# Second products 32 steps behind the first, w_in decoded first and without GpSimd, 25 attention batches ahead of the loop

## The chip, the core and the metric

The kernel runs on one core of a Trainium2 chip: TensorE (matrix products, into PSUM), VectorE and ScalarE (elementwise work, both read PSUM), GpSimd (elementwise work on SBUF), and SyncE, whose queue issues nearly all transfers between DRAM and SBUF. Each engine takes its instructions in the order in which the program gives them. The metric is the time of one execution in microseconds (us), the median of several.

## What is computed

A retention layer (attention with a decay in place of the softmax) over 8 sequences of 576 tokens and 8 heads of 64, and two MLPs on its 4608 tokens, with 512 inputs and 2048 inner columns each:

```
scores = (q @ k.T) / sqrt(64)                       # per batch and head
ret    = (scores * where(i >= j, gamma_h ** (i - j), 0)) @ v
x = ret, heads side by side                         # 4608 x 512
h = x @ w_in;   x = (h * sigmoid(1.702 * h)) @ w_out    # first MLP
h = x @ w_in2;  y = (h - tanh(h)) @ w_out2              # second MLP
```

The weights reach the kernel as 64-bit floats, so that it must turn them into 32-bit values itself; this is called decoding here.

## The kernel before, in words

**Pieces.** Each operand of a large product is split into a high part and a low rest (`xh`, `xl`; the halves of `wi`, `wos` and `g`), and three products of parts are summed. The tokens come in 9 blocks of 512, the inner columns in 16 groups of 128. A step `s` is one block `j` and one group `f` of one MLP, 288 in all. In a step `mm_in` (L356 to L367) makes the first product `h` in 12 matmuls of 512 columns, `act_a` (L369) the activation `t` out of it (a tanh on ScalarE and one instruction on VectorE in the first MLP, three and five in the second), `act_b` (L388) splits `t` into `g` (a copy on ScalarE, a subtraction on VectorE), and `mm_out` (L394 to L407) adds the second product of the step `LAG` = 2 steps ago to four PSUM accumulators, in 12 matmuls. `evac` (L409) empties these after 16 steps: into DRAM after the first MLP, from where `x2_load` and `x2_split` take the block for the second, into the output after the second.

**Attention.** A batch is half a tile of 128 tokens (four heads); there are 72, 8 to a block. Each has scores (L251), a state (L266), the part of the result from the state (L237) and from the masked scores `p` (L302). VectorE makes `p` (L274), the new state (L284 or L288) and `xl` (L317), ScalarE `xh` (L316) and the state's copy `sbd` (L324). `at_scale` (L201) scales queries and keys of a tile on GpSimd, L209 and L212. Nine batches stand ahead of the main loop, the others go in at every second step, as late as the blocks allow.

**Decoding.** There are 64 chunks of 128 x 512 values: two MLPs, 16 groups, `w_in` (c = 0) and `w_out` (c = 1), which take turns. A chunk is loaded by `wload` (L94), then goes through `dec_a` (VectorE L104, ScalarE Relu L106, VectorE L107), `dec_a2` (VectorE L112), `dec_b` (VectorE L118, GpSimd multiplication L123) and `dec_c` (ScalarE copy L139, GpSimd subtraction L140). `dec_piece` hands these out in thirds of a chunk, three chunks being in work at a time. During the first block each step takes two chunks, since each step needs its own `wi` and its own `wos`; the second MLP's chunks follow later, one every three steps, and go to DRAM. The 16 `wi` stay in SBUF; `wos` are stored to DRAM too and loaded again for each later block by `wo_load` (L177), through a ring of 4 buffers, on SyncE's queue.

**Order.** The order of instructions on each engine is the one in which the program writes them. PSUM has `pat` (2 banks), two `h` (1 each) and four accumulators; ahead of the loop three pairs of banks `pe` stand in place of `h` and the accumulators.

Of the kernel before, what the change touches and what calls it, by code (L numbers as in the profile page):

```python
# [16 lines left out]
P = 128  # L17
# [22 lines left out]
N_WARM = 12  # L40


@with_exitstack
def kernel(
# [12 lines left out]
    LAG = 2  # L57
# [3 lines left out]
    wos_p = ctx.enter_context(tc.tile_pool(name="wos", bufs=4))  # L61
    x_p = ctx.enter_context(tc.tile_pool(name="x", bufs=2))
    at_p = ctx.enter_context(tc.tile_pool(name="at", bufs=2))
    p_p = ctx.enter_context(tc.tile_pool(name="p", bufs=4))
    g_p = ctx.enter_context(tc.tile_pool(name="g", bufs=LAG + 1))
# [3 lines left out]
    ps_a = ctx.enter_context(tc.tile_pool(name="ps_a", bufs=1, space=bass.MemoryType.PSUM))  # L69

# [45 lines left out]
    def dec_b(m, f, c):  # L116
# [6 lines left out]
        nc.gpsimd.tensor_tensor(out=o, in0=z.bitcast(F32), in1=e.bitcast(F32), op=ALU.mult)  # L123
        half[m, f, c] = o

    def dec_c(m, f, c):
        o = half.pop((m, f, c))
        if c == 1:
            if m == 0:
                s = wos[f] = wos_p.tile([P, 2, DM], F32R, tag="wos", name="wos")  # L130
            else:
                s = st_p.tile([P, 2, DM], F32R, tag="stg", name="w2s", bufs=3)
        elif m == 0:
            s = wts.tile([P, 2, KD, P], F32R, tag=f"wi{f}", name="wi")
            win[f] = s
        else:
            s = st_p.tile([P, 2, KD, P], F32R, tag="stg", name="w2s", bufs=3)
        sv = s if c == 1 else s.rearrange("p a k c -> p a (k c)")
        nc.scalar.activation(out=sv[:, 0], in_=o, func=ACTF.Copy)  # L139
        nc.gpsimd.tensor_tensor(out=sv[:, 1], in0=o, in1=sv[:, 0].bitcast(F32), op=ALU.subtract)  # L140
        if c == 1 or m == 1:
# [4 lines left out]

    chunks = []
    for m in range(2):
        for f in range(NF + 1):
            chunks += ([(m, f, 0)] if f < NF else []) + ([(m, f - 1, 1)] if f else [])  # L150
# [8 lines left out]
    def dec_piece():  # L159
        n, k = divmod(n_dec[0], 3)  # L160
        if n >= len(chunks) + 2:
            return
        n_dec[0] += 1
        if k == 0:
            dec_load(n + 2)
            if n >= 2:
                dec_c(*chunks[n - 2])
            if 1 <= n <= len(chunks):
                dec_b(*chunks[n - 1])
        elif n < len(chunks):  # L170
            (dec_a if k == 1 else dec_a2)(*chunks[n])

    def dec_slot():
        for _ in range(3):
            dec_piece()
# [150 lines left out]
    def attn_step(b, ps=None):  # L326
# [4 lines left out]
        if now:  # L331
# [3 lines left out]
            if early:  # L335
                bat_p(b)
# [238 lines left out]
```

## Time and profile before

| | us |
|---|---|
| median of 3 executions (1793.1 to 1794.53) | 1793.56 |
| the profiled execution | 1794.65 |
| its span in the trace | 1792.9 |
| TensorE busy in the span | 1749.3 (98%) |
| VectorE busy | 1076.5 (60%) |
| ScalarE busy | 717.9 (40%) |
| GpSimd busy | 329.4 (18%) |

The shares are means over stages that differ, so they are to be read by stretches. In rows of the trace PE is TensorE, PEld its weight loads, DVE VectorE, ACT ScalarE, POOL GpSimd, SPq SyncE's queue. Every row names a line of the kernel before, what is written `<-` what is read, and a duration. A bracket at the end of a row is the idle time of the engine before it, and whose work ended that.

### The profile page before, as it was taken

To read this page: it belongs to the slowest core of one execution; us is meant where nothing else is said; L and a number is where in the kernel's file an instruction comes from. 1 tells how busy PE (TensorE), PEld (TensorE's weight loads), DVE (VectorE), ACT (ScalarE), POOL (GpSimd) and SP (SyncE) were. 2 spreads that over 40 slices of the span, in tenths; PEclk is the share of its full clock that TensorE was granted. 3 is DMA by queue.
4 is the path that set the end of the run, shared out by engine and by line. 5 is a ranking of instruction groups with operands and counts; after the bars stand their busy time and mean duration, and the time that the engine had idled before them with its cause. 6 is when DMAs were issued, how large, how long until landed. Compare 5 with 4: busy or idle time off the path is not lost.

```text
span 1792.9 us, 22946 instructions
## 1 busy us (share of the span) xinstructions
PE 1749.3 (98%) x8920; PEld 1430.8 (80%) x8920; DVE 1076.5 (60%) x1690; ACT 717.9 (40%) x1299; POOL 329.4 (18%) x240
## 2 busy tenths in 40 slices
PE   7878999999999999999999999999999999999999
PEld 5656788888888888888888888888888888888887
DVE  6899744444444445433322577777777777777776
ACT  2434433333333323323222444454445444545444
POOL 4666422223223223210001010101000000000000
PEclk7988999999999999999999999999999999999999
DMA  5555745555455545633355524342434233424232
GB/s 215 169 188 187 259 165 179 185 188 203 155 218 186 186 158 189 222 127 133 119 197 190 188 95 141 103 144 94 141 100 147 94 141 99 148 95 141 95 129 83
DMA packets 75421, 277.63 MB, mean 155 GB/s; under 512 B 8752, under 2 KB 8880, under 8 KB 69680
## 3 DMA queue, kind: packets, MB, share of 16 engines
q1 hardware_dynamic: 74736, 276.07, 44.0%
q8 instruction: 71, 1.16, 0.3%
q14 instruction: 38, 0.31, 0.1%
q10 hardware_dynamic: 576, 0.08, 0.0%
HBM read 232.08 MB, written 44.04 MB: 154 GB/s over the span
## 4 chain that ended last, share of the span: by engine, by line
PE 90%; DVE 8%; issue 1%; DMA 0%; ACT 0%; POOL 0%; SPq 0%; DVEq 0%; POOLq 0%
PE h L364 41%; PE acc L407 22%; PE acc L405 20%; DVE z L107 2%; PE pat L251 2%; DVE g L392 2%; PE pat L302 1%; DVE e L118 1%; PE pat L237 1%; PE pat L266 1%; DVE e L104 1%; DVE t L374 1%; DMA at<-in_attn_dram 0%; DVE z L112 0%; DVE p L274 0%
## 5 line engine op out<-in xcount | busy, mean ns | idle before, releaser
L364 PE MATMUL h<-xh,wi 128*128 128x512 f32 x2304 | 768.6, 395 | 28.6 <-ACT wi L139 22.2
L364 PEld LDWEIGHTS h<-xh,wi 128*128 128x128 f32 x2304 | 437.6, 190 | 129.2 <-ACT wi L139 25.7
L364 PE MATMUL h<-xl,wi 128*128 128x512 f32 x1152 | 453.2, 393 | 0.0
L405 PE MATMUL acc<-g,wos 128*128 128x512 f32 x1728 | 424.1, 394 | 0.6 <-DVE g L392 0.5
L407 PE MATMUL acc<-wos,g 128*128 128x512 f32 x1728 | 415.0, 389 | 0.0
L405 PEld LDWEIGHTS acc<-g,wos 128*128 128x128 f32 x1728 | 319.4, 188 | 75.6 <-issue 9.4
L407 PEld LDWEIGHTS acc<-wos,g 128*128 128x128 f32 x1728 | 324.1, 188 | 67.8 <-DVE g L392 0.4
L392 DVE TENSOR_TENSOR g<-t,g 128x512 fp32r<-128x512 f32 x288 | 238.3, 827 | 209.4 <-ACT g L391 209.4
L391 ACT ACTIVATE g<-t 128x512 fp32r<-128x512 f32 x288 | 181.3, 630 | 433.1 <-DVE t L386 354.4
L364 PEld LDWEIGHTS h<-xl,wi 128*128 128x128 f32 x1152 | 219.3, 190 | 45.6
L374 DVE SCALAR_TENSOR_TENSOR t<-t,h 128x512 f32<-128x512 f32 x144 | 98.3, 682 | 157.4 <-ACT t L373 156.9
L438 POOL TENSOR_TENSOR xl<-x2s,xh 128x512 fp32r<-128x512 f32 x36 | 46.5, 1293 | 774.2 <-ACT xh L437 774.2
L381 DVE TENSOR_TENSOR t<-h,t 128x512 f32<-128x512 f32 x144 | 99.6, 692 | 98.1 <-ACT sq L379 98.1
L373 ACT ACTIVATE t<-h 128x512 f32<-128x512 f32 x144 | 86.0, 598 | 173.4 <-PE h L364 172.1
L317 DVE TENSOR_TENSOR xl<-pat,xh 128x256 fp32r<-128x256 f32 x64 | 27.1, 423 | 208.2 <-ACT xh L316 208.2
L140 POOL TENSOR_TENSOR w2s<-z,w2s 128x512 fp32r<-128x512 f32 x32 | 53.8, 1683 | 383.9 <-ACT w2s L139 383.9
L316 ACT ACTIVATE xh<-pat 128x256 fp32r<-128x256 f32 x64 | 24.5, 382 | 238.6 <-PE pat L302 238.6
L386 DVE COPY_PREDICATED t<-sq,pl 128x512 f32<-128x512 int32 x144 | 109.2, 759 | 4.9
L123 POOL TENSOR_TENSOR z<-z,e 128x512 f32<-128x512 f32 x64 | 100.1, 1564 | 35.3 <-DVE e L118 35.3
L380 ACT ACTIVATE pl<-sq,abias 128x512 f32<-128x512 f32 x144 | 104.1, 723 | 4.8
L383 DVE SCALAR_TENSOR_TENSOR pl<-pl,sq 128x512 f32<-128x512 f32 x144 | 99.7, 692 | 9.4
L378 ACT ACTIVATE t<-h 128x512 f32<-128x512 f32 x144 | 86.1, 598 | 42.8 <-PE h L364 42.8
(61 smaller groups left out, 1174.6 us busy)
## 6 DMA issues: line engine op xcount, KB each, us to landing
wos<-wd SPq DMA_DIRECT2D x272, 512.0 KB, 4.4
at<-in_attn_dram SPq DMA_DIRECT2D x35, 1024.0 KB, 4.9
stg<-in_w_dram SPq DMA_DIRECT2D x64, 512.0 KB, 5.5
wd<-w2s SPq DMA_DIRECT2D x32, 512.0 KB, 3.0
x<-o SPq DMA_DIRECT2D x36, 256.0 KB, 3.6
x2s<-x SPq DMA_DIRECT2D x9, 1024.0 KB, 6.7
out_dram<-o SPq DMA_DIRECT2D x36, 256.0 KB, 2.3
wd<-wos SPq DMA_DIRECT2D x16, 512.0 KB, 2.9
```

The lines of the kernel that those rows point to most:

```text
L123: nc.gpsimd.tensor_tensor(out=o, in0=z.bitcast(F32), in1=e.bitcast(F32), op=ALU.mult)
L364: nc.tensor.matmul(h, lhsT=win[f][:, a, k], rhs=xs[b][:, k], start=(n == 0), stop=(n == 3 * KD - 1))
L374: nc.vector.scalar_tensor_tensor(out=t, in0=t, scalar=1.0, in1=h, op0=ALU.add, op1=ALU.mult)
L378: nc.scalar.activation(out=t, in_=h, func=ACTF.Tanh)
L380: nc.scalar.activation(out=pl, in_=sq, func=ACTF.Square, bias=abias)
L381: nc.vector.tensor_tensor(out=t, in0=h, in1=t, op=ALU.subtract)
L383: nc.vector.scalar_tensor_tensor(out=pl, in0=pl, scalar=CB, in1=sq, op0=ALU.add, op1=ALU.mult)
L386: nc.vector.copy_predicated(out=t, mask=sq.bitcast(I32), data=pl)
L391: nc.scalar.activation(out=g[:, 0], in_=t, func=ACTF.Copy)
L392: nc.vector.tensor_tensor(out=g[:, 1], in0=t, in1=g[:, 0].bitcast(F32), op=ALU.subtract)
L405: nc.tensor.matmul(acc[m], lhsT=wo[:, a, c], rhs=g[:, b], start=first, stop=last)
L407: nc.tensor.matmul(acc[m], lhsT=g[:, a, c], rhs=wo[:, b], start=first, stop=last)
```

## The change

- `LAG` grows from 2 to 32 steps. The first 32 first products are issued without a second one. An activation `t` is stored to DRAM by `g_store`, and loaded back two steps ahead of its second product by `g_load`; `act_b` then works on the loaded tile `gl`.
- The chunks go through the decode in another order: the 16 of the first `w_in`, then the first `w_out`, then the second MLP's two. All but the first 16 go to DRAM through two buffers `ws`, and every `wos` is loaded.
- The two GpSimd instructions of the decode move to VectorE; the last is a part of its own (`dec_d`). The decode goes on until step 89: three pieces a step in the first ten steps after step 32, then two.
- 25 batches instead of 9 stand ahead of step 32, in a ring of three PSUM buffers (`pat` and two `pe`) beside two `h`; there the state's part of the result comes behind the scores.
- The tables `mt_sb` are made on ScalarE; 12 of 24 first matmuls on zeros are left out.
- The last 32 steps have second products only. The weights of the last two blocks are loaded once, into the places of the `wi` (`wo_stay`), and the last block's accumulators are `pat` and two `h`.
- Rings: `wos` 3 instead of 4, `x` 3 instead of 2, `p` 3 instead of 4, `g` 2 instead of 3, `t` 3 instead of 2.

The diff, cut to its core:

```diff
+LAG = 2 * NF
+RING = 3
+EARLY = 3 * BPB + 1
...
-        nc.gpsimd.tensor_tensor(out=o, in0=z.bitcast(F32), in1=e.bitcast(F32), op=ALU.mult)
+        nc.vector.tensor_tensor(out=o, in0=z.bitcast(F32), in1=e.bitcast(F32), op=ALU.mult)
...
     def dec_c(m, f, c):
-        o = half.pop((m, f, c))
...
+        o = half[m, f, c]
+        if (m, c) == (0, 0):
+            s = win[f] = wts.tile([P, 2, KD, P], F32R, tag=f"wi{f}", name="wi")
+            sv = s.rearrange("p a k c -> p a (k c)")
         else:
+            sv = st_p.tile([P, 2, DM], F32R, tag="ws", name="ws", bufs=2)
         nc.scalar.activation(out=sv[:, 0], in_=o, func=ACTF.Copy)
-        nc.gpsimd.tensor_tensor(out=sv[:, 1], in0=o, in1=sv[:, 0].bitcast(F32), op=ALU.subtract)
+        half[m, f, c] = o, sv
+
+    def dec_d(m, f, c):
+        o, sv = half.pop((m, f, c))
+        nc.vector.tensor_tensor(out=sv[:, 1], in0=o, in1=sv[:, 0].bitcast(F32), op=ALU.subtract)
+        if (m, c) != (0, 0):
             d = dram.tile([P, 2 * DM], F32, tag=f"w{m}{f}{c}", name="wd")
...
+    chunks = [(m, f, c) for m in range(2) for c in range(2) for f in range(NF)]
...
+            if k == 1 and n >= 2:
+                dec_d(*chunks[n - 2])
+            if n < len(chunks):
+                (dec_a if k == 1 else dec_a2)(*chunks[n])
...
+    def attn_early(b, ps):
+
+        bat_qk(b, ps, False)
+        if b:
+            bat_sq(b - 1)
+        bat_state(b)
+        bat_p(b)
+        if b:
+            bat_pv(b - 1)
+            bat_x(b - 1)
+        attn_next(b)
...
+    def g_store(s):
+        gd[s] = dram.tile([P, BLK], F32, tag=f"g{s % (LAG + NF)}", name="gd")
+        nc.sync.dma_start(out=gd[s], in_=tt.pop(s))
+
+    def g_load(s):
+        t = gl[s] = t_p.tile([P, BLK], F32, tag="gl", name="gl")
+        nc.sync.dma_start(out=t, in_=gd.pop(s))
...
+        for f in range(NF):
+            mm_in(f)
+            if f < NF // 2:
+                dec_piece(3)
+                act_a(f)
+                early(BPB + 1 + f)
+            else:
+                s = NF + 2 * (f - NF // 2)
+                g_store(s - 1 if f > NF // 2 else f - 1)
+                mm_in(s)
+                dec_piece(2)
+                act_a(f)
+                early(BPB + 1 + f)
+                dec_piece()
+                act_a(s)
+                g_store(f)
+                mm_in(s + 1)
+                dec_piece(2)
+                act_a(s + 1)
+                g_store(s)
+            if 0 < f < NF // 2:
+                g_store(f - 1)
...
+    for s in range(LAG, n_steps + LAG):
+        j, f = divmod(s, NF)
+        o = s - LAG
+        if o == 0:
+            g_store(s - 1)
             for i in range(2):
...
+                wo_load(i)
+                g_load(i)
+            act_b(0)
         if s < n_steps:
             mm_in(s)
+        if s < n_steps + LAG - 1:
+            act_b(o + 1)
+        if s % 2 == 0 and EARLY + (s - LAG) // 2 <= TILES * BPT:
+            attn_step(EARLY + (s - LAG) // 2)
+        dec_piece()
         if s < n_steps:
             act_a(s)
...
+        if s < n_steps + LAG - 2:
+            wo_load(o + 2)
+            g_load(o + 2)
+        if o and s <= n_steps:
+            g_store(s - 1)
+        mm_out(o)
+        dec_piece(2 if j == 2 and f < 10 else 1)
+        if f == NF - 1:
+            evac(o)
```

How this moves instructions is seen at three places. The first is VectorE's queue in the first block. Before, one step without attention (from `t` of one step to `t` of the next) held two chunks, whose last two instructions were on GpSimd:

```order
L374 SCALAR_TENSOR_TENSOR t_735<-t_735,h_698 128x512
L118 SCALAR_TENSOR_TENSOR e_692<-stg_667,e_692 128x512
L104 TENSOR_SCALAR e_759<-stg_685 128x512
L107 TENSOR_SCALAR z_760<-stg_685 128x512
L112 SCALAR_TENSOR_TENSOR z_760<-stg_685,z_760 128x512
L392 TENSOR_TENSOR g_765<-t_735,g_765 128x512
L118 SCALAR_TENSOR_TENSOR e_759<-stg_685,e_759 128x512
L104 TENSOR_SCALAR e_775<-stg_750 128x512
L107 TENSOR_SCALAR z_776<-stg_750 128x512
L112 SCALAR_TENSOR_TENSOR z_776<-stg_750,z_776 128x512
```

Now, in one of the first eight steps, there is one chunk, with its multiplication (L125) and its subtraction (L140), and one batch (L280, L294, L323); L106, L109, L114 and L120 are the old L104, L107, L112 and L118, and L397 is the old L374:

```order
L106 TENSOR_SCALAR e_470<-stg_406 128x512
L109 TENSOR_SCALAR z_471<-stg_406 128x512
L397 SCALAR_TENSOR_TENSOR t_475<-t_475,h_449 128x512
L280 TENSOR_TENSOR p_483<-pe_478,mt_sb_93 128x512
L294 SCALAR_TENSOR_TENSOR s_sb0_102<-s_sb0_102,gt_sb_97,pe_478 128x64 x2
L323 TENSOR_TENSOR xl_444<-pat_104,xh_443 128x2x128
L114 SCALAR_TENSOR_TENSOR z_471<-stg_406,z_471 128x512
L120 SCALAR_TENSOR_TENSOR e_470<-stg_406,e_470 128x512
L125 TENSOR_TENSOR z_471<-z_471,e_470 128x512
L140 TENSOR_TENSOR wi_527<-z_414,wi_527 128x512
```

The two instructions L125 and L140 have come into VectorE's queue, `g` has left it for these steps, and `t` stands right behind the two masks.

The second place is ScalarE's queue in the same steps, now. `e` is the Relu of a chunk (L108, the old L106), `t` the tanh (L396, the old L373):

```order
L322 ACTIVATE xh_443<-pe_478 128x2x128
L330 ACTIVATE sbd0_100<-s_sb0_102 64x2x64 x2
L135 ACTIVATE wi_581<-z_471 128x512
L108 ACTIVATE e_586<-e_586,ebias_98 128x512
L396 ACTIVATE t_591<-h_565 128x512
L322 ACTIVATE xh_443<-pe_540 128x2x128
```

The tanh stands right behind the Relu, which waits for VectorE's first mask of the same chunk.

The third place is SyncE's queue in the first MLP. Before, with one chunk in three steps (`wos` is a weight load, `wd<-w2s` the store of a decoded chunk):

```order
L180 DMA wos_4103<-wd_613 128x1024
L94 DMA stg_4121<-in_w_dram 128x512
L143 DMA wd_4126<-w2s_4123 128x1024
L180 DMA wos_4155<-wd_672 128x1024
L180 DMA wos_4212<-wd_755 128x1024
L180 DMA wos_4245<-wd_814 128x1024
```

Now, from the hand-over at step 32 on (`gd<-t` is the store of an activation, `gl<-gd` its load, `wd<-ws` the store of a chunk):

```order
L413 DMA gd_1639<-t_1630 128x512
L179 DMA wos_1641<-wd_1309 128x1024
L417 DMA gl_1643<-gd_509 128x512
L179 DMA wos_1645<-wd_1357 128x1024
L417 DMA gl_1647<-gd_563 128x512
L96 DMA stg_1692<-in_w_dram 128x512
L179 DMA wos_1701<-wd_1420 128x1024
L417 DMA gl_1703<-gd_620 128x512
L143 DMA wd_1722<-ws_1694 128x1024
L96 DMA stg_1746<-in_w_dram 128x512
```

Where a step had one weight load, and a chunk now and then, it has a weight load, an activation's load and an activation's store, and in the first ten of these steps a chunk each.

## Rows read from the trace of the kernel before

**Rows 1.** Stretches: bounds in us, length, busy time per engine, PEclk, DMA share, GB/s.

```profile
0.00:42.00 42.00, 30.66 (x256) 22.38 (x256) 26.04 (x61) 11.34 (x29) 16.17 (x21) 0.76 0.59 221
42.00:201.84 159.84, 131.56 (x661) 99.83 (x661) 153.31 (x194) 66.73 (x126) 102.79 (x73) 0.89 0.57 186
201.84:1008.00 806.16, 806.16 (x4562) 662.72 (x4561) 330.44 (x576) 256.53 (x504) 169.11 (x115) 1.00 0.50 179
1008.00:1793.00 785.00, 780.92 (x3444) 645.89 (x3443) 566.71 (x861) 383.27 (x643) 41.37 (x32) 1.00 0.35 120
```

**Rows 2.** Timeline, first block: start us, length us, engine, line, operation [idle before].

```profile
75.24 0.73 PE L364 MATMUL h<-xh,wi 128*128 128x512 f32 x2 [0.75 <-POOL wi L140]
75.66 0.68 DVE L118 SCALAR_TENSOR_TENSOR e<-stg,e 128x512 int32<-128x512 int32 x1
...
76.41 1.41 POOL L123 TENSOR_TENSOR z<-z,e 128x512 f32<-128x512 f32 x1 [1.23 <-DVE e L118]
76.59 1.52 DVE L107 TENSOR_SCALAR z<-stg 128x512 int32<-128x512 int32 x1
...
82.76 1.40 POOL L140 TENSOR_TENSOR wi<-z,wi 128x512 fp32r<-128x512 f32 x1 [0.74 <-ACT wi L139]
...
82.95 1.76 DVE L392 TENSOR_TENSOR g<-t,g 128x512 fp32r<-128x512 f32 x1
...
84.63 0.68 DVE L118 SCALAR_TENSOR_TENSOR e<-stg,e 128x512 int32<-128x512 int32 x1
```

**Rows 3.** Timeline from 711 us, VectorE and ScalarE; GpSimd idle until 714.44.

```profile
711.04 0.42 DVE L317 TENSOR_TENSOR xl<-pat,xh 128x256 fp32r<-128x256 f32 x1 [5.00 <-ACT xh L316]
...
711.54 0.60 ACT L373 ACTIVATE t<-h 128x512 f32<-128x512 f32 x1
...
712.36 0.68 DVE L374 SCALAR_TENSOR_TENSOR t<-t,h 128x512 f32<-128x512 f32 x1
712.96 0.69 DVE L118 SCALAR_TENSOR_TENSOR e<-stg,e 128x512 int32<-128x512 int32 x1
...
713.56 0.42 DVE L104 TENSOR_SCALAR e<-stg 128x512 int32<-128x512 int32 x1
...
713.89 0.42 DVE L107 TENSOR_SCALAR z<-stg 128x512 int32<-128x512 int32 x1
...
714.26 0.71 ACT L106 ACTIVATE e<-e,ebias 128x512 int32<-128x512 int32 x1
...
714.35 0.69 DVE L112 SCALAR_TENSOR_TENSOR z<-stg,z 128x512 f32<-128x512 uint32 x1
...
714.88 0.62 ACT L391 ACTIVATE g<-t 128x512 fp32r<-128x512 f32 x1
```

**Rows 4.** Timeline of TensorE, first product to first product, 713 to 727 us.

```profile
713.36 0.39 PE L364 MATMUL h<-xh,wi 128*128 128x512 f32 x1
...
716.08 2.88 PE L405 MATMUL acc<-g,wos 128*128 128x512 f32 x12
...
718.80 0.39 PE L364 MATMUL h<-xh,wi 128*128 128x512 f32 x1
...
726.37 0.39 PE L364 MATMUL h<-xh,wi 128*128 128x512 f32 x1
```

**Rows 5.** Timeline: the start of first product 0, and of first product 18.

```profile
42.01 0.80 PE L364 MATMUL h<-xh,wi 128*128 128x512 f32 x1 [0.94 <-DVE xl L317]
...
201.84 0.39 PE L364 MATMUL h<-xh,wi 128*128 128x512 f32 x1
```

**Rows 6.** Groups by line: scaling on GpSimd; busy us, mean ns, idle before.

```profile
L209 POOL TENSOR_TENSOR at<-at,qt_sb 128x512 f32<-128x512 f32 x35 | 46.1, 1316 | 114.8 <-DMA at<-in_attn_dram 114.8
```

**Rows 7.** Stretches: a busy one behind the first block, columns as in Rows 1.

```profile
200.00:240.00 40.00, 40.00 (x229) 32.41 (x228) 20.06 (x35) 15.30 (x30) 14.92 (x11) 1.00 0.71 251
```

**Rows 8.** Transfers, weight loads in 200:240 and 1600:1700: count, KB, median us to landing.

```profile
wos<-wd SPq DMA_DIRECT2D x8, 512.0 KB, 6.8
...
wos<-wd SPq DMA_DIRECT2D x18, 512.0 KB, 3.3
```

More of the change, by code (lines that the diff above doesn't have):

```diff
@@ L188, in at_load @@
     def at_load(t):
-        if t < TILES:
+        if t < TILES and t not in at:
             if t in (2, 3):
@@ L324, in bat_x, with attn_next, attn_step @@
             nc.scalar.activation(out=sbd[bt][r, :, r], in_=s_sb[bt][r], func=ACTF.Copy)
-    def attn_step(b, ps=None):
-        now, before = 0 <= b < TILES * BPT, 0 <= b - 1 < TILES * BPT
-        early = ps is not None
+    def attn_next(b):
+        t, bt = divmod(b, BPT)
+        if bt == 0:
+            if t >= TPB - 1:
+                at_load(t + 1)
+            at_scale(t + 1)
+        elif t in (1, 2):
+            at_load(t + TPB - 1)
+    def attn_early(b, ps):
[8 more added lines that the diff above has]
+        attn_next(b)
+    def attn_step(b):
+        now, before = b < TILES * BPT, b - 1 < TILES * BPT
         opened = bat_sq(b - 1) if before else False
         if now:
-            t, bt = divmod(b, BPT)
-            bat_qk(b, ps if early else pat, opened and not early)
+            bat_qk(b, pat, opened)
             bat_state(b)
-            if early:
-                bat_p(b)
         if before:
@@ L340, in attn_step @@
         if now:
-            if not early:
-                bat_p(b)
-            if bt == 0 and t >= TPB - 1:
-                at_load(t + 1)
-            if bt == (0 if t < TPB - 1 else 1):
-                at_scale(t + 1)
+            bat_p(b)
+            attn_next(b)
     hps = {}
+    tt = {}
+    gd = {}
+    gl = {}
     gt = {}
@@ L490 @@
-    ps_h = ctx.enter_context(tc.tile_pool(name="ps_h", bufs=2, space=bass.MemoryType.PSUM))
+        for _ in range(N_WARM):
+            nc.tensor.matmul(pat[:, 1], lhsT=warm[:, 0:P], rhs=warm, start=True, stop=True)
+        for b in range(BPB + 1):
+            if b < BPT:
+                for hp in (2 * b, 2 * b + 1):
+                    at_scale(0, hp)
+                for i in range(2):
+                    for k in range(2):
+                        h = 2 * (2 * b + k) + i
+                        nc.scalar.activation(
+                            out=mt_sb[:, b, i, k], in_=mk_sb, func=ACTF.Copy, scale=jt_sb[:, h:h + 1]
+                        )
+            early(b)
+            dec_piece(int(b > 0))
@@ L491 @@
     ps_acc = ctx.enter_context(tc.tile_pool(name="ps_acc", bufs=1, space=bass.MemoryType.PSUM))
     n_steps = 2 * NB * NF
[L494 removed]
+    for s in range(LAG, n_steps + LAG):
         j, f = divmod(s, NF)
[L496 to L499 removed]
+        o = s - LAG
+        if o == 0:
+            g_store(s - 1)
+            for i in range(2):
+                wo_load(i)
+                g_load(i)
+            act_b(0)
```

118 lines of the change are left out of this document (38 added, 80 removed).

## The prediction

> **What bounds the kernel now.** I read the stretches first, then single instructions inside them. In the stretches [rows 1] the reader should see two programs. From 201.84 us on, TensorE is busy without a gap, at full granted clock (1.00, the level of 2.4 GHz), and only the last microseconds are idle. Before that it is not: 30.66 of the first 42.00 us and 131.56 of the next 159.84, at a mean granted clock of 0.76 and 0.89, so part of that work ran at the lower level. VectorE is busy 153.31 us of those 159.84, so in this stretch VectorE is the bound and TensorE waits, in the end for weights: the idle time before a first product at 75.24 was ended by GpSimd's write of `wi` [rows 2].
>
> Why VectorE is so slow there is read from single instructions. The decode of a weight chunk has four VectorE instructions and two on GpSimd. In [rows 2] the masking at L107 takes 1.52 us while a GpSimd multiplication of 1.41 us that began 0.18 us ahead of it runs; the subtraction at L392 takes 1.76 us beside one that began 0.19 ahead of it. In [rows 3], where no GpSimd instruction runs, the same L107 takes 0.42. So the two engines take turns, and GpSimd's work costs VectorE about its own length. Two chunks, one `t` and one `g` took from 75.66 to 84.63, 8.97 us.
>
> At the full clock a first product takes 2.72 us (713.36 to 716.08), a step without attention 5.44 (713.36 to 718.80) and one with a batch 7.57 (718.80 to 726.37), so a batch costs TensorE 2.13 [rows 4]. At 201.84 [rows 5] 18 first products (216 matmuls), 16 second products and 18 batches had been issued: (18+16) x 2.72 + 18 x 2.13 = 131 us of work. Some 70 us are there to be won, and nothing after.
>
> **The change, part by part.** Until its step 32 the new program issues 25 batches and 32 first products, 25 x 2.13 + 32 x 2.72 = 140 us for TensorE, and no second product. Call T the moment at which first product 32 starts.
>
> *Nine batches ahead of the first product.* They stay, with nearly the same decode pieces between them. The tables move from VectorE to ScalarE; the next state still waits for GpSimd's scaling. First product at 42.0 as now [rows 5]; between 38 and 46.
>
> *Products 0 to 7, one chunk and one batch each.* VectorE's spacing from start to start [rows 3]: a two-input instruction 0.60 (712.96 to 713.56), the mask 0.33, the second mask with its wait 0.46. A chunk now has four of the first kind, two of them GpSimd's before: 4 x 0.60 + 0.33 + 0.46 = 3.2, with a wait between the dependent ones 3.3. The two have no VectorE row; I take 0.60 because they are 512-column instructions with two inputs like the one beside them, and the bounds are 0.33 and the 0.69 that one lasts. Attention takes 1.32 (711.04 to 712.36), `t` 0.60. The order shows a new wait: the tanh stands right behind the chunk's Relu on ScalarE, and `t` right behind the masks on VectorE, so VectorE waits for 0.71 + 0.60 less the second mask's 0.33, about 1.0 [rows 3]. The scaling on GpSimd stays: one instruction of 1.3 us per batch [rows 6]; VectorE reads no PSUM in about half of its time, so 0.5 (0 to 1.3). Sum 6.7, times 8 is 54 us. TensorE needs 4.85, at the 0.89 of [rows 1] 5.4, so VectorE sets the pace; at the lower level throughout TensorE would need 9.7, and 78 us is the upper bound.
>
> *Products 8 to 31, three with one batch and five thirds of a chunk.* VectorE: 5.5 + 1.8 + 1.3 + 1.2 of such waits (some are filled by the next instruction) + 0.5 = 10.3. TensorE: 3 x 2.72 + 2.13 = 10.3. Two engines with equal loads and two `h` buffers between them wait for each other: 10.3 if they interleave perfectly, 12.4 if VectorE also waits out the batch's 2.13 on TensorE. I take 11.2, nearer the first, because only the scores and the result of a batch are waited for, and first products can run ahead. Times 8 is 90 us. T = 42 + 54 + 90 = 186, from 174 to 206.
>
> *The rest.* Before, 1591.1 us were left at 201.84. From T there are 14 first products fewer, 16 second products more and 7 batches fewer: -38.1 + 43.5 - 14.9 = -9.5.
>
> *The hand-over at step 32.* SyncE's queue reaches the first weight and `g` loads only behind the store of activation 31, and the first `act_b` waits for them. Landing 3.3 to 6.8 us [rows 8] and 0.62 + 0.69 of conversion (a copy, and an instruction like L112) [rows 3], less 2.72 + 2.13 of work that TensorE has meanwhile: 0 to 6, I take 4.
>
> *The round trip through DRAM.* 288 stores and 288 loads of 256 KB are added to SyncE's queue, behind waits for second products. A load is issued when the step before last's product ends, a whole step ahead of its conversion and two ahead of its use, over 10 us against 6.8 for twice the size in a busy stretch [rows 8]. The weight ring shrinks from four to three, the `p` ring too; a weight load still has 13 us. VectorE's and ScalarE's work per step does not grow. So nothing in the steady state. Without that cover each step would pay a landing.
>
> *Steps 32 to 89, where decode goes on.* Weights 0.52 MB, `g` out and in 0.52, attention 0.26, and per chunk 1.05 give 2.36 MB a step at three pieces (10 steps) and 2.01 at two (48 steps): 120 MB in 58 x 6.5 = 377 us, 318 GB/s. A busy stretch of 40 us now moves 251 GB/s at a share of 0.71 [rows 7], 354 at a full one. The first ten steps ask for 363. I take 3 us, 0 to 20.
>
> *The last 32 second products without first ones.* A `g` buffer cycle: 0.62 + 0.69 + at most 3.3 for the load, since that is what twice the size took on a quiet queue [rows 8], is 4.6 against the 5.44 of two products. Nothing; 0 to 10.
>
> Sum: 186 + 1591.1 - 9.5 + 4 + 3 = 1774.6 us of span. The profiled execution is 1794.65 for a span of 1792.9, 1.75 more, and lies 1.1 above the median: **1775 us**.
>
> **Where a rule speaks against it.** VectorE is nearly full and is given more work. The Trainium skill, page "Perfetto Trace Analysis", section "Optimizing Scalar/DVE Operations", says that a saturated VectorE may be helped by giving work to ScalarE or even GpSimd, and adds that between GpSimd and VectorE it might not help, since they share a port. By the rule's first half this change goes the wrong way, and by its second it does not; the masks with and without GpSimd beside them [rows 2, 3] are on the side of the second. The first half is rival 3, whose price follows from the rows.
>
> **The rivals.**
> 1. *The early stretch runs better.* If scaling costs VectorE nothing and the two engines interleave without waits, products 0 to 7 take 50 and 8 to 31 take 82: T = 174, and without losses behind it 1757 to 1765. For it: VectorE was 96% busy in the stretch now. Against: the Relu-tanh wait stands in the order.
> 2. *It runs worse, with TensorE at its lower level.* TensorE has spare time in products 0 to 7, and in the first 42 us such spare time went with a clock of 0.76 [rows 1]. Then products 0 to 7 take 62 to 70, of the 78 at most, and 8 to 31 some 95: T = 199 to 207, and 1788 to 1796.
> 3. *GpSimd did help.* If the long masks have another cause than GpSimd, each of 24 chunks keeps its 1.1 + 0.8 us of excess and the gain of T is gone: 1.9 x 24 = 46, 1820. Against it stands 0.42 without GpSimd [rows 3].
> 4. *The transfers become the bound in steps 32 to 89; slower.* 120 MB need 318 GB/s. If stores and loads mixed sustain only 290, these steps last 414 instead of 377 us, VectorE waits for `stg` and ScalarE for `ws`, TensorE for both: 1772 + 37 = 1809. It decides from 318 down, and brings the kernel above its old time at 301. For it: that stretch was already 71% busy [rows 7]. Against: the remaining 29% would carry the demand but for the first ten steps.
> 5. *It doesn't do what it says*: second products still meet late activations, because SyncE's queue is in order and one late wait delays all loads. At 0.08 us a step over 256 steps the gain is gone, 1795.
>
> **How the numbers follow.** The forecast (1766 to 1785) has 0.60, rival 1 0.14, rival 2 0.11, rival 3 0.02, rival 4 0.08, rival 5 0.05. The range is 1758 to 1793: it leaves out the upper part of 2, all of 3 and 4, and the best of 1. About 0.2%, 3.6 us, can be told from no change: faster 0.83 (forecast, 1 and most of 2), same 0.07 (the rest of 2, most of 5), slower 0.10 (3 and 4).
>
> **What would show it.** Right: the masks at 0.42 throughout; first product 32 starts near 186 us; VectorE near full until then, with a wait of about 1 us before `t` for the tanh; TensorE full and at 1.00 from about 195 us to the end, steps of 5.44 and 7.57. Wrong: masks above 1 us with GpSimd idle (3); a granted clock under 0.8 between 42 and 100 (2); TensorE idle between 190 and 570 us with `stg`, `ws` or `gl` as releasers and a DMA share over 0.9 (4); idle time before second products later on, ended by `g` (5). A gap in the last 90 us would show that the single load per product is too slow.

## The result: slower by 1.0%, and the profile after

The changed kernel takes **1812.08 us** (median of four runs, 1808.02 to 1814.83) against 1793.33 for the kernel before, measured in turn with it: a ratio of **1.0104**, 95% interval 1.0079 to 1.0129. The forecast was 1775, with 1758 to 1793 as its range, so the time lies outside it and on the other side. The profiled execution of the changed kernel took 1809.77 us for a span of 1808.0.

The stretches of the changed kernel answer to [rows 1], cut at the start of first product 32 (columns as there):

```profile
0.00:42.00 42.00, 33.29 (x303) 23.34 (x304) 28.74 (x66) 17.11 (x44) 13.84 (x19) 0.92 0.64 234
42.00:174.80 132.80, 121.50 (x767) 90.62 (x766) 110.78 (x203) 50.96 (x109) 18.39 (x13) 0.99 0.62 208
174.80:600.00 425.20, 397.28 (x2230) 318.86 (x2232) 258.38 (x472) 145.81 (x294) 36.48 (x28) 0.96 0.85 292
600.00:1808.00 1208.00, 1200.67 (x5618) 991.29 (x5614) 672.50 (x1072) 497.97 (x860) 64.03 (x51) 1.00 0.65 221
```

The trouble has moved. In the second row TensorE is busy 121.50 of 132.80 us at a granted clock of 0.99, where before it had 0.89; the early stretch is better than forecast. The third row is new: TensorE idle for 28 us at a mean clock of 0.96, in steps where before, behind 201.84, it had no gap. VectorE is busy for 258 of those 425 us and the DMA engines for 0.85, so neither is full.

TensorE's timeline of the changed kernel (start, length, engine, line, operation) gives the bounds of that loss: the first of products 0 and 8, then the last of product 31 and the first of product 32 in one row, the first of product 33, the first of product 90:

```profile
32.83 0.50 PE L387 MATMUL h<-xh,wi 128*128 128x512 f32 x1
...
81.84 0.50 PE L387 MATMUL h<-xh,wi 128*128 128x512 f32 x1
...
174.41 0.89 PE L387 MATMUL h<-xh,wi 128*128 128x512 f32 x2
...
190.92 0.63 PE L387 MATMUL h<-xh,wi 128*128 128x512 f32 x1
...
595.80 0.39 PE L387 MATMUL h<-xh,wi 128*128 128x512 f32 x1
```

Product 32 starts at 174.8 (T in the prediction). Its step lasts 16.1 us, 8.6 more than the 7.57 of [rows 4]. Steps 33 to 89 take 404.9 us; in an experiment below without a gap in them they take 368.5. So 36.4 us are lost there, and some 5 at the end, and 11 were gained at T. These steps in the two kernels, the changed one first (columns as above), show what the 36.4 are made of:

```profile
190.92:595.80 404.88, 382.57 (x2146) 307.34 (x2144) 249.59 (x456) 140.33 (x283) 34.21 (x26) 0.97 0.85 292
191.46:559.98 368.52, 368.44 (x2145) 302.58 (x2144) 256.03 (x459) 143.36 (x285) 37.90 (x26) 1.00 0.90 325
```

TensorE is idle for 22.3 us, and the same work keeps it busy 14.1 us longer, at a mean clock of 0.97 in place of 1.00.

Where TensorE waits in steps 33 to 89, it waits for `g` (made from `gl`) at some steps, and for `o`, the evacuation copy, at others. Its waits for these from 185 to 600 us (waiting line, releaser: us in total, times, longest; the 5.6 is that of the hand-over):

```profile
PE acc L439 <- ACT o L449: 15.1, 5, 5.0
PE acc L439 <- ACT g L422: 9.0, 4, 5.6
```

So `o` ends most of the idle time, 15.1 us, and `g` 3.4 behind the hand-over. The waits of SyncE's queue in the same stretch show what both have to do with each other:

```profile
SPq L143 <- DVE ws L140: 218.8, 41, 8.3
SPq L204 <- PE pat L308: 19.1, 8, 4.6
```

For 218.8 of 415 us SyncE stood at L143, the store of a decoded chunk, until VectorE had written `ws`. Whatever comes behind it in program order stood there too, without a row of its own.

### The profile page after: what moved, and what is told of

Its sections match the earlier page's. It is cut to its first block, busy times and chain, and to the rows that moved or that the text cites. A ratio compares the mean times of both kernels' runs of the same rounds, so it can differ in the third digit from the quotient of the medians.

```text
span 1808.0 us, 24474 instructions
## 1 busy us (share of the span) xinstructions
PE 1752.8 (97%) x8908; PEld 1424.1 (79%) x8908; DVE 1070.4 (59%) x1810; ACT 711.9 (39%) x1307; POOL 132.7 (7%) x111
## 4 chain that ended last, share of the span: by engine, by line
PE 79%; DMA 8%; DVE 7%; ACT 2%; issue 2%; SPq 1%; ACTq 0%; DVEq 0%
PE h L387 36%; PE acc L441 20%; PE acc L439 18%; DMA gl<-gd 7%; PE pat L441 1%; PE pat L257 1%; DVE t L397 1%; DVE p L280 1%; PE pat L308 1%; DVE e L120 1%; DVE ws L140 1%; PE pat L243 1%; SPq L179 1%; ACT g L422 1%; DMA x<-o 1%
## 5 line engine op out<-in xcount | busy, mean ns | idle before, releaser
L439 PE MATMUL acc<-g,wos 128*128 128x512 f32 x1728 | 433.1, 399 | 25.3 <-ACT o L449 15.1
L423 DVE TENSOR_TENSOR g<-gl,g 128x512 fp32r<-128x512 f32 x288 | 198.4, 689 | 392.3 <-ACT g L422 392.1
L439 PEld LDWEIGHTS acc<-g,wos 128*128 128x128 f32 x1728 | 324.9, 191 | 104.8 <-ACT o L449 17.0
L422 ACT ACTIVATE g<-gl 128x512 fp32r<-128x512 f32 x288 | 181.9, 632 | 508.5 <-DMA gl<-gd 324.4
L441 PE MATMUL acc<-wos,g 128*128 128x512 f32 x1344 | 322.8, 389 | 0.0
L441 PEld LDWEIGHTS acc<-wos,g 128*128 128x128 f32 x1344 | 252.2, 188 | 52.4
L397 DVE SCALAR_TENSOR_TENSOR t<-t,h 128x512 f32<-128x512 f32 x144 | 98.3, 683 | 62.0 <-ACT t L396 61.8
L108 ACT ACTIVATE e<-e,ebias 128x512 int32<-128x512 int32 x64 | 46.4, 725 | 170.8 <-DVE e L106 170.8
L407 DVE SCALAR_TENSOR_TENSOR pl<-pl,h 128x512 f32<-128x512 f32 x144 | 98.9, 687 | 4.9
L396 ACT ACTIVATE t<-h 128x512 f32<-128x512 f32 x144 | 84.4, 586 | 37.3 <-PE h L387 36.7
L215 POOL TENSOR_TENSOR at<-at,qt_sb 128x512 f32<-128x512 f32 x35 | 46.8, 1337 | 694.8 <-DMA at<-in_attn_dram 582.8
L402 ACT ACTIVATE sq<-h 128x512 f32<-128x512 f32 x144 | 85.4, 593 | 0.0
```

The source lines that it names most:

```text
L397: nc.vector.scalar_tensor_tensor(out=t, in0=t, scalar=1.0, in1=h, op0=ALU.add, op1=ALU.mult)
L407: nc.vector.scalar_tensor_tensor(out=pl, in0=pl, scalar=C2, in1=h, op0=ALU.mult, op1=ALU.mult)
L422: nc.scalar.activation(out=g[:, 0], in_=t, func=ACTF.Copy)
L423: nc.vector.tensor_tensor(out=g[:, 1], in0=t, in1=g[:, 0].bitcast(F32), op=ALU.subtract)
L439: nc.tensor.matmul(acc[m], lhsT=wo[:, a, c], rhs=g[:, b], start=first, stop=last)
L441: nc.tensor.matmul(acc[m], lhsT=g[:, a, c], rhs=wo[:, b], start=first, stop=last)
```

## One turn of the ring

The timeline of the changed kernel from 375 to 393 us, SyncE's issues with ScalarE, VectorE and the first matmul of a second product (in brackets the idle time before, and who ended it):

```profile
375.41 1.09 SPq L417 DMA_DIRECT2D gl<-gd  x1
...
377.05 0.52 SPq L96 DMA_DIRECT2D stg<-in_w_dram  x1
...
383.88 0.63 ACT L422 ACTIVATE g<-gl 128x512 fp32r<-128x512 f32 x1 [6.79 <-DMA gl<-gd]
384.54 0.69 DVE L423 TENSOR_TENSOR g<-gl,g 128x512 fp32r<-128x512 f32 x1 [4.95 <-ACT g L422]
...
385.15 0.68 DVE L140 TENSOR_TENSOR ws<-z,ws 128x512 fp32r<-128x512 f32 x1
...
385.92 0.32 SPq L143 DMA_DIRECT2D wd<-ws  x1
386.63 0.32 SPq L179 DMA_DIRECT2D wos<-wd  x1
387.01 0.54 SPq L417 DMA_DIRECT2D gl<-gd  x1
...
392.00 0.63 ACT L422 ACTIVATE g<-gl 128x512 fp32r<-128x512 f32 x1 [4.59 <-DMA gl<-gd]
...
392.69 0.50 PE L439 MATMUL acc<-g,wos 128*128 128x512 f32 x1 [1.49 <-ACT g L422]
```

Read it from the top. A `gl` load issued at 375.41 lands at 383.9. VectorE stood 4.95 us at L423 for it, and the chunk's `ws` (L140) stands behind L423 in VectorE's order, so it is begun at 385.15. SyncE, whose last issue ended at 377.57, has been standing at the store of that chunk, which starts at 385.92; the next `gl` load is behind the store and is issued at 387.01. It lands 5 us later, and for TensorE this is 1.49 too late. Late `gl`, late `g`, late `ws`, late store, late `gl`: the lateness of one load is handed to the next. The Trainium skill, "Perfetto Trace Analysis", section "DMA Instruction — HWDGE (DVE, Sync)", says that the semaphore wait of a DMA lies with the issuing sequencer and ahead of the profiled time; the trace agrees, since the time from 377.57 to 385.92 has no row in SyncE's timeline and is seen in the waits alone (8.3 us, the longest of the 41).

The gaps by `o` look like another matter. Here are ScalarE's instructions around the evacuation copies, the `o` stores and the second product behind them, in the timeline of the changed kernel:

```profile
295.43 0.63 ACT L422 ACTIVATE g<-gl 128x512 fp32r<-128x512 f32 x1 [5.11 <-DMA gl<-gd]
297.76 0.72 ACT L108 ACTIVATE e<-e,ebias 128x512 int32<-128x512 int32 x1 [1.70 <-DVE e L106]
...
298.87 1.56 ACT L449 ACTIVATE o<-acc 128x512 f32<-128x512 f32 x3
299.51 3.23 PE L439 MATMUL acc<-g,wos 128*128 128x512 f32 x9 [2.49 <-ACT o L449]
299.70 8.36 SPq L450 DMA_DIRECT2D x<-o  x4
307.12 0.60 ACT L449 ACTIVATE o<-acc 128x512 f32<-128x512 f32 x1 [6.69 <-DMA x<-o]
307.77 1.65 PE L439 MATMUL acc<-g,wos 128*128 128x512 f32 x3 [5.03 <-ACT o L449]
```

There are two kinds of them. TensorE's 2.49 us stand before the first matmul of the product: the copies stand in ScalarE's order behind a `g` that waited 5.11 us for its `gl`, and behind a Relu (L108) that waited 1.70 more for VectorE, so this gap is the late `gl` again. The 5.03 us stand before its tenth matmul: three copies fill the three buffers of the ring `p`; the fourth waits 6.69 us until the first store has landed, and TensorE waits for the accumulator. That made the smaller ring the first suspect, and bandwidth the second: from 200 to 400 us the DMA share was 0.84 to 0.92.

## The experiments

Three theories: A, the ring `p` with three buffers; B, SyncE's order; C, the transfers themselves. D is the hand-over at step 32. A time is a median of four runs (of ten where half of the weight loads are left out), and a ratio is against the kernel before, timed again beside each group of kernels (1791.18 to 1793.67), with its 95% interval; "less" is against the 1812.08 of the changed kernel.

**The ring `p` (A).**

```diff
-    p_p = ctx.enter_context(tc.tile_pool(name="p", bufs=3))
+    p_p = ctx.enter_context(tc.tile_pool(name="p", bufs=4))
```

> The `p` ring gets its fourth buffer back; nothing else changes. Theory A (the ring: the fourth `o` copy of an evacuation waits for the store of the first, and TensorE waits for the accumulator): the gaps at steps 48-49, 64 and 80-81 cost 10.3 + 6.1 + 6.2 = 22.6 us beyond 5.44 and 7.57 a step in the changed kernel; most of it goes, so 15 to 23 us less than the changed kernel, 1789 to 1797 us, and no TensorE gap above 1 us is ended by L449. Theories B (SyncE's in-order queue is held up by the chunk stores) and C (transfers at a DMA share of 0.8 to 0.9 land too late): the ring only hands on their lateness; the late `gl` gaps stay, and the time falls by under 8 us, 1804 or more.

1805.89, ratio 1.0080 (1.0059 to 1.0101): 6 us less, with intervals that overlap. The gaps before a tenth matmul are gone, so the ring has its part in those. Gaps of 2.16 and 3.53 us ended by L449, both before a first matmul, are still there, one by `g` of 1.60 at 563 us is new, and the waits for `t` grow from 2.4 to 7.0 us. A is at most a small part.

**The chunk stores on another queue (B against C).**

```diff
-            nc.sync.dma_start(out=d, in_=sv.rearrange("p a n -> p (a n)").bitcast(F32))
+            nc.gpsimd.dma_start(out=d, in_=sv.rearrange("p a n -> p (a n)").bitcast(F32))
```

> The chunk stores `wd<-ws` are issued by GpSimd's queue, which is nearly idle there, and not by SyncE's; same bytes. Theory B (SyncE's in-order queue stands at each chunk store until VectorE has written `ws`, 219 us in all, and the `gl` loads and `o` stores behind it are issued late): gaps ended by `gl` at steps 40-46, 60-62, 73-74 (4.5 + 4.6 + 3.8 us) go, and the `o` stores start sooner: 15 to 35 us less than the changed kernel, 1777 to 1797. Theory C (bytes): SyncE waits less, but landings stay at 5.5 to 8 us and the time stays within 6 us, 1806 to 1818. Theory A: the gaps before L449 stay nearly as they are; 8 to 13 us less.

1780.77, ratio 0.9942 (0.9923 to 0.9961): **31 us less**, and faster than the kernel before. Its stretches 200:260 and 260:320, in both of which TensorE has no idle time:

```profile
200.00:260.00 60.00, 60.00 (x370) 49.66 (x369) 48.18 (x88) 24.34 (x49) 9.55 (x12) 1.00 0.95 345
260.00:320.00 60.00, 60.00 (x345) 49.00 (x344) 41.03 (x74) 24.46 (x50) 10.59 (x12) 1.00 0.96 351
```

Its `gl` loads from 200 to 570 us, in the list of transfers (count, KB, median us to landing):

```profile
gl<-gd SPq DMA_DIRECT2D x56, 256.0 KB, 7.7
```

The same stretches of the changed kernel:

```profile
200.00:260.00 60.00, 59.18 (x365) 47.92 (x366) 43.85 (x80) 22.34 (x44) 5.51 (x4) 1.00 0.92 318
260.00:320.00 60.00, 51.27 (x277) 39.90 (x275) 34.78 (x64) 21.20 (x44) 4.03 (x3) 0.91 0.84 289
```

and its `gl` loads, from the same list:

```profile
gl<-gd SPq DMA_DIRECT2D x51, 256.0 KB, 6.3
```

With the stores gone from SyncE's queue, more bytes per second move (345 and 351 GB/s against 318 and 289), and a `gl` load takes longer to land, 7.7 us against 6.3. The rate of 289 was not what the transfers could do, but what they were asked for. C falls as the cause. (Three gaps by `o`, of 0.32 to 2.46 us, remain behind 390 us, two of them before a tenth matmul.)

**One piece a step from step 42 on.**

```diff
-        dec_piece()
+        if s < 3 * NF - 6:
+            dec_piece()
         if s < n_steps:
             act_a(s)
```

> From step 42 on one piece of a chunk is decoded per step and not two; the last chunk is then ready some 40 steps later, still before it is loaded. Both the chunk stores in SyncE's queue and the chunk traffic per step are halved. Theories B and C alike: 1.05 MB x 1/3 less per step, some 260 GB/s asked instead of 318; gaps at steps 48 to 85 (10.3 + 4.6 + 6.1 + 3.8 + 6.2 + .8 = 32 us) fall to a third or less: 1785 to 1795. Theory A (ring alone): the `o` gaps remain, 23 us, and the time stays above 1800.

1777.85, ratio 0.9927 (0.9912 to 0.9942): 34 us less, more than expected. It goes with B and C alike; it only shows that the chunks are the place.

**Fewer weight bytes.** Of the second products 0 to 57 every second one gets no weight load of its own and uses the tile of the step before.

```diff
+        if o % 2 and o < 58:
+            wos[o] = wos[o - 1]
+            return
         t = wos[o] = wos_p.tile([P, 2, DM], F32R, tag="wos", name="wos")
```

> Leaves out every second weight load of the second products 0 to 57, which then use the tile of the step before (so those products are computed with the wrong weights): 0.26 MB a step less of some 2, with chunk decode, queue order and rings as they are. Theory C (bytes): asked rate falls from 318 to some 278 GB/s, landings of `gl` fall from 5.5-8 us towards 4, and most of the 32 us of gaps at steps 48 to 85 goes: 1780 to 1795. Theory B (SyncE held by chunk stores): the waits at the chunk stores stay, gaps stay: within 6 us of the changed kernel, 1806 to 1818.

1790.07, ratio 0.9993 (0.9980 to 1.0006): 22 us less, in C's range; but C's reason for it did not show, since `gl` still lands in 6.0 us in the median (6.1 in the changed kernel, both from 185 to 600), and SyncE still stands 211 us at the chunk store. The run takes away both bytes and an issue ahead of half of the `gl` loads (in the changed kernel a `wos` issue lasts 0.32 to 1.84 us, 0.42 in the median), and does not tell which of the two helped.

**The place in the queue alone.** The strictest test of B: same queue, bytes, buffers and number of issues; two lines are moved up in the step.

```diff
         if s < n_steps + LAG - 1:
             act_b(o + 1)
+        if s < n_steps + LAG - 2:
+            wo_load(o + 2)
+            g_load(o + 2)
...
-        if s < n_steps + LAG - 2:
-            wo_load(o + 2)
-            g_load(o + 2)
```

> In each step the loads of `wos` and `gl` for the second product after next are issued before the step's decode pieces and attention, not behind them; same queue, same bytes, same number of issues, same buffers. Theory B as it stands now (a ring of waits: `gl` late, so `g` on VectorE late, so the chunk's `ws` behind it late, so the chunk store on SyncE late, so the next `gl` behind it late): the store no longer stands between them, and 25 to 35 us go, 1777 to 1787, although the waits at the chunk store remain. Theory C (bytes, or SyncE issuing too many transfers): nothing of that changes, 1804 or more.

1774.52, ratio 0.9901 (0.9882 to 0.9919): **38 us less**, the most of the single edits. The waits of SyncE's queue in this kernel (185 to 600):

```profile
SPq L143 <- DVE ws L140: 138.1, 41, 7.3
```

and TensorE's first matmuls of products 33 and 90 in its timeline:

```profile
191.46 0.39 PE L387 MATMUL h<-xh,wi 128*128 128x512 f32 x1
...
559.98 0.39 PE L387 MATMUL h<-xh,wi 128*128 128x512 f32 x1
```

SyncE still stands 138 us at the same stores, and from step 42 on two of three loads still come behind one; but it is that of the step before, and no longer that of the load's own step. (In the ten steps ahead, with three pieces each, it is that of the step before in the changed kernel too, and there, from 200 to 260 us, TensorE is idle for only 0.8 us.) Steps 33 to 89 take 368.5 us, without a wait of TensorE. The transfers move 352 and 341 GB/s in the two stretches above, on the same queue. The gaps by `o` are gone too, with three buffers in the ring: those before a first matmul hung on the late `gl`; why those before a tenth go too was not separated (in the step of the rows above the first `o` store lands in 5.4 us here and in 7.4 there). B is shown. The loads also come ahead of the attention's load (L204) now, which stood 19.1 us in the changed kernel; what that is worth was not tried by itself, but it is not needed for the 31 us of the stores alone.

**More time for the load.** A third `gl` buffer, and the load three steps ahead, with SyncE's order as in the changed kernel.

```diff
-        t = gl[s] = t_p.tile([P, BLK], F32, tag="gl", name="gl")
+        t = gl[s] = t_p.tile([P, BLK], F32, tag="gl", name="gl", bufs=3)
...
-            g_load(o + 2)
+        if s < n_steps + LAG - 3:
+            g_load(o + 3)
```

> A third `gl` buffer, and each `gl` loaded three steps ahead of its use in place of two; SyncE's order, the chunk stores and the bytes stay. If what counts is the time a `gl` load has before its conversion, a whole step (5.4 to 7.6 us) more of it removes all gaps by `gl`, those by `o` that follow from it, and the 5.6 us at the end: 1775 to 1790. If SyncE stands still at the chunk store for other reasons than a late `gl` (VectorE late by itself), or if bytes bind, the gaps stay and only the end improves: 1804 to 1808.

1777.14, ratio 0.9918 (0.9897 to 0.9940): 35 us less. It cuts the ring at another link: the load is still issued late, but no conversion waits for it. The gaps by `g` in steps 33 to 89 and the gap in the last 90 us are gone. Three gaps by `o` (1.54, 2.91 and 2.77 us) stay, all before a tenth matmul, where the three buffers of `p` are full.

**Two mends for one cause.**

> The chunk stores on GpSimd's queue and one piece per step from step 42 on, together. If the two act on one cause (loads late because of what lies ahead of them, as queue position or as bytes), each has nearly taken it all (31 and 34 us) and together they give what is left without gaps: first product 32 at 175, 1581.6 behind it, 11.9 at the hand-over, 5.6 at the end, 1.75 around the span, 1773 to 1778. If they were two causes with prices of their own, the sum of 65 us would show, 1750 or less, below the time without any gap, which speaks against it beforehand.

Its edits are those of chunk_stores_off_sync and one_piece_per_step. 1774.21, ratio 0.9896 (0.9881 to 0.9910): 38 us less where 31 + 34 would have been 65. One cause, as expected.

**The hand-over (D).**

```diff
                 g_store(s - 1 if f > NF // 2 else f - 1)
+                if f == NF - 1:
+                    for i in range(2):
+                        if i < 2:
+                            wo_load(i)
+                        g_load(i)
...
             g_store(s - 1)
-            for i in range(2):
-                wo_load(i)
-                g_load(i)
             act_b(0)
```

> The first two loads of `wos` and `gl` are issued one product earlier, ahead of the stores of activations 30 and 31, in the last round of the product loop; all else as in the changed kernel. Theory D (at the hand-over the first `gl` waits behind the store of activation 31 in SyncE's queue, and the gap of 5.6 us also brings a lower granted clock for the product behind it, 5.8 in place of 2.9 us): 9 to 12 us less than the changed kernel, 1800 to 1803, no gap over 1 us near 185 and a granted clock of 1.00 there. Rival: the start of the second products only uncovers the next late load: the gap moves to the next products and under 4 us are gained, 1808 or more.

1807.22, ratio 1.0081 (1.0063 to 1.0099): 5 us less, between the two theories, and not told apart from none. The gap at the hand-over is gone in its trace, but the ring takes back what is won: gaps of 1.43 us at 239 and 5.49 at 418 stand where there were none and 3.59. Product 32 also began at 180 in that profile, which did not come again below (176.8). So it was tried again on top of loads_ahead.

> The loads before the step's pieces, as in loads_ahead (1774.5 us), and the first two loads of `wos` and `gl` before the stores of activations 30 and 31, as in handover_loads_early. If the hand-over costs what its rows show (10.5 us from product 32 to the first second product where 4.85 are work, and a product of 5.6 in place of 2.9: 8 to 9 us), and it was hidden in handover_loads_early only by the late loads behind it: 1764 to 1768. If the gap just moves on, or the early loads push the product loop back as its later start of product 32 (180 in place of 175) hinted: 1771 or more.

1765.95, ratio 0.9855 (0.9838 to 0.9871): 8.6 us below loads_ahead, which is what the rows of the changed kernel had said. These rows of the timeline:

```profile
177.68 0.32 SPq L413 DMA_DIRECT2D gd<-t  x1
178.05 0.72 SPq L179 DMA_DIRECT2D wos<-wd  x1
178.82 0.60 SPq L417 DMA_DIRECT2D gl<-gd  x1
...
184.66 0.63 ACT L422 ACTIVATE g<-gl 128x512 fp32r<-128x512 f32 x1 [7.73 <-DMA gl<-gd]
185.34 0.80 PE L439 MATMUL acc<-g,wos 128*128 128x512 f32 x1 [5.61 <-ACT g L422]
```

and the stretch behind the gap, of the changed kernel too:

```profile
185.00:191.40 6.40, 6.06 (x14) 4.46 (x15) 4.77 (x10) 2.81 (x7) 0.00 (x0) 0.50 0.60 235
```

The first `gl` is issued behind the store of activation 31, 4.0 us after product 32 began, and lands 5.8 us later. TensorE waits 5.61, and then runs the product (185.34 to 190.92, 5.58 us in place of 2.72) at a granted clock of 0.50, its lower level: the gap costs another 2.9 us, half its length, behind itself. (The 11.9 us that the expectation of the two mends gives the hand-over were too many; T to product 33 less 7.57 is 8.6.)

**The decode back on GpSimd.** The multiplication of L125 and the subtraction of L140 go back; all else as changed.

```diff
-        nc.vector.tensor_tensor(out=o, in0=z.bitcast(F32), in1=e.bitcast(F32), op=ALU.mult)
+        nc.gpsimd.tensor_tensor(out=o, in0=z.bitcast(F32), in1=e.bitcast(F32), op=ALU.mult)
...
-        nc.vector.tensor_tensor(out=sv[:, 1], in0=o, in1=sv[:, 0].bitcast(F32), op=ALU.subtract)
+        nc.gpsimd.tensor_tensor(out=sv[:, 1], in0=o, in1=sv[:, 0].bitcast(F32), op=ALU.subtract)
```

> The multiplication and the subtraction of the decode go back to GpSimd; all else as in the changed kernel. Theory of the prediction (GpSimd and VectorE take turns, a GpSimd instruction of 1.4 us costs VectorE its length, 0.6 on VectorE itself): 24 chunks before first product 32 with 2 x 0.8 us more each, T at 210 to 225 in place of 175, time 1840 to 1870; masks L107 at 1 us or more. Rival 3 (GpSimd helps): VectorE has 24 x 1.2 = 29 us less, T at 146 to 160, time 1783 to 1800.

1874.13, ratio 1.0450 (1.0433 to 1.0468): 62 us more. The masks from 42 to 175 us (busy us, mean ns) in this kernel:

```profile
L109 DVE TENSOR_SCALAR z<-stg 128x512 int32<-128x512 int32 x16 | 17.5, 1096 | 3.9 <-POOL wi L140 3.9
L106 DVE TENSOR_SCALAR e<-stg 128x512 int32<-128x512 int32 x16 | 12.4, 778 | 11.4 <-POOL z L125 11.4
```

and in the changed kernel:

```profile
L109 DVE TENSOR_SCALAR z<-stg 128x512 int32<-128x512 int32 x19 | 10.2, 538 | 0.0
L106 DVE TENSOR_SCALAR e<-stg 128x512 int32<-128x512 int32 x19 | 8.8, 464 | 0.0
```

The first matmuls of products 0 and 32 (the latter is the second one of its row) in this kernel's timeline:

```profile
33.68 0.50 PE L387 MATMUL h<-xh,wi 128*128 128x512 f32 x1
...
199.57 0.76 PE L387 MATMUL h<-xh,wi 128*128 128x512 f32 x2
```

First product 0 starts at 33.68 and product 32 at 199.8, 25 us later than in the changed kernel, less than the 35 to 50 expected; the other 37 us are lost behind T, where the ring has GpSimd in it too (SyncE stands 246.9 us at the chunk store from 215 to 660 us). That GpSimd's two instructions lengthen VectorE's masks is shown, and rival 3 of the prediction is out.

**All mends.** The two of SyncE, the hand-over, `p` with four buffers and the third `gl`:

> The chunk stores on GpSimd's queue, one piece per step from step 42, four `p` buffers, hand-over loads early, and a third `gl` buffer with the load three steps ahead. Without any gap: 175 + 1581.6 + 1.75 = 1758; with 0 to 6 us left: 1757 to 1765, about 30 us below the kernel before. If the late loads have a further cause that these leave, 1770 or more, with gaps before second products in the trace.

1761.01, ratio **0.9822** (0.9807 to 0.9837), 51 us less than the changed kernel and 33 less than the kernel before. Its stretch from 174.8 to 600:

```profile
174.80:600.00 425.20, 425.20 (x2486) 349.15 (x2486) 235.20 (x428) 150.04 (x299) 54.82 (x61) 1.00 0.79 287
```

TensorE is busy for all of 425.20 us at a clock of 1.00.

> As the kernel with all mends, but the chunk stores stay on SyncE's queue and the loads are issued before the step's pieces instead. If the place of the loads in the queue is the whole matter: 1758 to 1764, as with GpSimd's queue. If the stores must leave SyncE for it: 1766 or more, with gaps by `gl` between 190 and 300 us.

The same with the loads moved up as in loads_ahead, and the stores left on SyncE: 1761.06, ratio 0.9830 (0.9810 to 0.9850). The stores need not leave the queue; it is enough that a load does not stand behind the store of its own step.

## Why the prediction was wrong

*T, 11 us too late.* Forecast 186 (174 to 206), measured 174.8. The parts: first product 0 at 42 forecast and 32.8 measured, outside the 38 to 46; products 0 to 7 in 54, measured 49.0; products 8 to 31 in 90, measured 93.0. The last two were sized well, and the wait-free pace of rival 1 (82) did not come; its T of 174 was met because the nine batches ended 9 us sooner than "as now". The stretch from the third batch's scores (14.23 us before, 14.27 now) to product 0, before and now, columns as in [rows 1]:

```profile
14.20:42.00 27.80, 21.22 (x194) 16.66 (x192) 19.38 (x42) 10.06 (x28) 10.81 (x9) 0.68 0.43 166
14.20:32.80 18.60, 15.73 (x194) 12.45 (x192) 16.50 (x37) 8.65 (x24) 8.41 (x8) 0.91 0.59 216
```

The first 14 us are alike, so neither the tables on ScalarE nor the matmuls left out did it. Behind them the same 194 matmuls take 18.6 us in place of 27.8: TensorE waits 2.7 us for the state `s_sb` in place of 5.2, and its clock is 0.91 in place of 0.68. With the decode back on GpSimd product 0 starts at 33.7 too. So the new order in a batch, with the state's part behind the next scores, is the likely reason, but it was not tried by itself. Nor was the pace what the forecast made of it: VectorE was to be near full, and is busy for 110.78 of 132.80 us (TensorE for 121.50); the wait before `t` was to be 1.0, and is 0.4 (12.3 us over 30). That 49.0 and 93.0 lie near 54 and 90 is in part luck. The clock of rival 2 did not fall (0.99). The masks' mean is 464 and 538 ns where [rows 2] show 1.52 us for one; a long one is still met where GpSimd scales (1.53 us at 77.44), as the prediction had allowed for. The Trainium skill, "SBUF — State Buffer", section "SBUF: two separate sides", states that of certain VectorE instructions and a GpSimd one the first to start holds the shared ports for its whole length. The means with the decode back on GpSimd, 778 and 1096 ns, agree in so far as the masks are longer beside GpSimd; who started first was not counted.

*Hand-over, mis-sized: 4 forecast (0 to 6), 8.6 measured.* The forecast's own terms give 6.8 + 0.62 + 0.69 - 4.85 = 3.3 at most, so neither the 4 nor the 6 came out of them. The landing, 5.8, lay inside its bounds. The 4.85 us of cover were counted as if the load were issued when product 32 begins; it is issued 4.0 us later, since the store of activation 31 ahead of it waits for that activation. And the 2.9 us at the lower clock were left out.

*Steps 32 to 89, the step that failed: 3 forecast (0 to 20), 36.4 measured.* The failing sentence is the one on the round trip, "A load is issued when the step before last's product ends, a whole step ahead of its conversion". That is when its buffer is free. When it is issued is set by what is ahead of it on SyncE, and from step 42 on this is in two of three steps a chunk store, in one of them that of the same step, whose `ws` stands on VectorE behind that step's `g`. The load issued at 387.01 then had 3.5 us (its conversion began at 392.00, 1.49 too late) and not over 10, and the median landing is 6.3. The diff showed all three links, and each was looked at by itself; the loop was not followed round.

*The demand on the transfers was estimated well, and its end was wrong.* 354 GB/s at a full share was the estimate from [rows 7]; without the ring the transfers moved 345 and 351 at 0.95 and 0.96. Rival 4 named nearly the time that came, 1809, by luck and with the wrong mechanism: a rate of 290 GB/s is what the profile shows (292 in the third stretch), but as a result of the waits. Rival 5 named the mechanism, an in-order queue in which one late wait delays all loads, and had a chance of 0.05 and a price of 0.08 us a step over 256 steps; it was 36.4 / 57 = 0.64 over 57, and none behind them, where no chunk is stored.

*The smaller rings.* "The `p` ring too" was passed over. With its fourth buffer alone TensorE's waits for `o` fall from 15.1 us to 5.7, and the time by only 6 us, within the uncertainty; with the loads ahead three buffers leave no gap.

*The last 32 second products, 0 forecast.* A 2.30 us gap before L441, ended by a late `gl`, in the timeline:

```profile
1718.47 0.63 ACT L422 ACTIVATE g<-gl 128x512 fp32r<-128x512 f32 x1 [5.46 <-DMA gl<-gd]
1719.15 5.58 PE L441 MATMUL acc<-wo,g 128*128 128x512 f32 x15 [2.30 <-ACT g L422]
```

and a lower clock in the stretch behind it:

```profile
1720.60:1724.00 3.40, 3.40 (x10) 2.65 (x9) 0.47 (x1) 0.06 (x1) 0.00 (x0) 0.50 0.60 154
```

From product 90 to the end the changed kernel took 1212.2 us, the kernel with all mends 1207.5 (550.23 to 1757.7): 4.7 us, within the 0 to 10.

Together, against the forecast span of 1774.6: -11.2 + 4.6 + 33.4 + 4.7 = +31.5, and the span is 33.4 longer; the other 1.9 lie in the steps that were taken as free of gaps.

## What to carry to other kernels

When an edit puts a transfer on the way of every step, write down for its issue not when its buffer is free but which instruction stands before it in the issuing queue, what that one waits for, and what stands before *that* on its engine; if the path comes back to the transfer, it is a ring, and each late turn makes the next one late. A store that waited for a slow engine belonged behind the loads of its step or on another queue here, and moving two lines was worth 38 us. A high DMA share beside idle engines is no proof of a full DMA: look whether the same bytes move faster when they are asked for sooner.

## What was not expected of the hardware

Behind each gap of over 2 us in steps 32 and later of the changed kernel, TensorE's granted clock fell to 0.50, the lower of its two levels, before it rose again: behind 5.61 us of waiting the product took 5.58 us in place of 2.72, and the stretch shows 0.50; behind the 5.03 us it is 0.50 from 306.92 to 310.92, behind the 3.59 from 418.92 to 422.92. In the kernel with all mends the clock is 1.00 from 174.8 on, but for its last instructions. Behind the gap of 2.30 us near the end 3.40 us pass at 0.50. Here an edit that closed such a gap was worth more than the gap's length: the 36.4 us of steps 33 to 89 are 22.3 of idle time and 14.1 of slower work.
